# A list scheduler that orders a fused attention and two-MoE kernel: own-engine waits, separate small tasks and a mode for turned blocks

## The chip, the cores and the metric

The kernel runs on one core of a Trainium2 chip. The metric is device time in microseconds (us) of one execution; lower is better. In the profile PE is the matmul engine, PEld its weight loads, DVE the vector engine, ACT the scalar engine, POOL GpSimd and SP the engine that issues most of the DMAs.

## The reference

Block-causal attention (blocks of 64) feeds a layer of three maxima, and that feeds a routed mixture of experts:

```python
# attention: B, H, S, D = 4, 8, 576, 64
scores = np.where(block_i >= block_j, scale * (q @ k.T), -1e9)
attn = np.exp(scores - scores.max(-1)); attn /= attn.sum(-1) + 1e-9
x = heads_side_by_side(attn @ v)                   # 2304 x 512
# first layer, d_ff 768
h = np.maximum(np.maximum(x @ w1, x @ w2), x @ w3)
x = h @ w_out
# second layer: 8 experts, 1024 wide, one expert for each token with x @ w_skip > 0
out = x; out[do] = x[do] + gate * (np.maximum(x[do] @ w1[e], 0) @ w2[e])
```

## The kernel before

The 2304 tokens are cut into six chunks of 384. For each chunk the attention runs in units: one pair of heads (four pairs) and one run of up to 128 query rows. A unit's steps are `s_scores` (PE, scores into `sc`), `s_max` (DVE, negated row maxima into `nm`), `s_exp` (ACT, `p` and its sums), `s_sum` (DVE, reciprocal of the sums into `r`), `s_norm` (ACT or DVE, `p` times `r`), `s_trans` (PE, blocks of `p` turned by a product with the identity, into `tp`), `s_turned` (copy of `tp` into `pT`), `s_pv` (PE, into `pv`) and `s_out` (ACT and DVE, the high and low part of `x`). Each product of the first layer is made of three float32r products of high and low parts. Per chunk it is 18 groups `mh` of 12 matmuls into `ps_h`, three groups `my` of 18 into `ps_y`, and routing (`ps_l`, `ps_r`, `ps_k`). The first layer's weights arrive as 64-bit words in 24 pieces. Each piece is decoded once: `ab` on ACT, four steps `dec` on DVE of which each reads what the one before wrote, then `hi` (ACT) and `lo` (DVE). The last six pieces are `w_out`; each is also turned (`pswt`) and multiplied by the routing weights (`psw`).

The attention of chunk c+1 is woven into the first layer of chunk c. So the program falls into: attention of chunk 0 alone; first layer of chunk 0 with the decoding and the attention of chunk 1; first layers of chunks 1 to 4 with the attention of chunks 2 to 5; first layer of chunk 5, while the first expert weights are loaded (`load_raws`) and split into high and low parts (lines 1032 and 1036); then the experts.

All but the last two parts are ordered by the class `Plan`: `build` describes each step as a `Task` with its engine, a duration, a due time `at` and what it needs; `order` plays the list through, engine by engine, and the tasks are then emitted in order of planned start. Each engine's queue runs in that order on the chip. The tables that the planner has of waits are `LATE` (from a task's end to a task on another engine) and `TURN` (when PE changes between full tiles F, two row halves R of `s_scores` and two column halves C of `s_pv`). The planner decides at each step by

```python
s, t = min(((s, t) for s, t in cand if s <= first + 0.05), key=lambda x: x[1].at)
```

Of the kernel before, what the change touches and what calls it, by code (L numbers as in the profile page):

```python
# [8 lines left out]
F32 = mybir.dt.float32  # L9
# [49 lines left out]
class Plan:  # L59
# [3 lines left out]
    TURN = {("F", "R"): 0.10, ("R", "F"): 0.10, ("F", "C"): 0.11, ("C", "F"): 0.15, ("C", "R"): 0.15, ("R", "C"): 0.2}  # L63
# [11 lines left out]
    def ready(self, t, eng):  # L75
        when = 0.0
        for d in t.deps:
            if d.end is None:
                return None
            when = max(when, d.end + (0.0 if d.on == eng else self.LATE[d.on]))  # L80
        for name in t.acq:
            n = len(self.allocs[name]) + t.acq.count(name) - self.bufs[name]
            for k in range(max(n - t.acq.count(name), 0), n):
                for d in self.allocs[name][k].releases_of[name]:
                    if d.end is None:
                        return None
                    when = max(when, d.end + (0.0 if d.on == eng else self.LATE[d.on]))
        return when

    def order(self):  # L90
# [14 lines left out]
        while todo:  # L105
            best = None
            for e in free:
                first, cand = None, []
                for t in todo:
                    if e in t.eng:  # L110
                        r = self.ready(t, e)
                        if r is not None:
                            s = max(r, free[e])
                            cand.append((s, t))
                            first = s if first is None else min(first, s)
                if first is None:
                    continue
                s, t = min(((s, t) for s, t in cand if s <= first + 0.05), key=lambda x: x[1].at)
                if best is None or s < best[0]:
                    best = (s, t, e)  # L120
# [6 lines left out]
            if e == "PE":  # L127
                t.end += self.TURN.get((mode, t.mode), 0.0)
                mode = t.mode
# [24 lines left out]
def build(S, E, groups, units):  # L154
# [14 lines left out]
    for u in units:  # L169
# [3 lines left out]
        when.append((c - 1) * span + (-6 if c == 0 else 0) + 0.8 * span * n / per[c])  # L173
# [27 lines left out]
    for ks in su:  # L201
# [9 lines left out]
        for n, k in enumerate(ks):  # L211
# [6 lines left out]
            mx = S.add("DVE", one * (parts if sets == 2 else 1) + 0.07 * parts, at - 2, lambda k=k: E.mx(k), [sc])  # L218
# [6 lines left out]
            rs = S.add("DVE", 0.16, at - 3, lambda k=k: E.rs(k), exs)  # L225
            nms = []
            for j in range(sets):
                nm = S.add(dict(ACT=0.19 + 0.83e-3 * nk, DVE=0.13 + 0.52e-3 * nk), 0, at - 2.5 + 0.1 * j, None, [rs])
# [4 lines left out]
            for m in range(0, todo, 4):  # L233
# [3 lines left out]
                           ["tp"] + (["pT"] if m == 0 else []))  # L237
# [43 lines left out]
    for k in range(18 + NF):  # L281
        at = first_w + w_pace * k if k < 18 else 8 + 5.0 * (k - 18)
# [132 lines left out]
def _moe1_phase(tc, nc, const, small, g):  # L415
# [11 lines left out]
    with ExitStack() as st_y:  # L427
# [187 lines left out]
        def s_sum(k):  # L615
# [8 lines left out]
            nc.vector.reciprocal(r[:, 0:sets], r[:, 0:sets])  # L624
# [50 lines left out]
        E.load, E.load_v, E.sc, E.mx, E.ex, E.rs, E.nm = load, load_v, s_scores, s_max, s_exp, s_sum, s_norm  # L675
# [622 lines left out]
```

## Time and profile before

| | |
|---|---|
| median of 3 runs | 664.79 us (664.69 to 665.62) |
| profiled execution | 664.43 us, span of its instructions 662.6 us |
| around the span | 1.83 us |
| PE busy | 616.7 us (93%) |
| DVE busy | 388.5 us (59%) |
| ACT busy | 325.4 us (49%) |
| mean granted TensorE clock | 0.971 |

PE is busy nearly throughout. The granted clock is 1.0 (2.4 GHz) in most of the span and 0.5 (1.2 GHz) in some stretches. A busy share over the whole span mixes parts that differ: decoding of weights happens in the first 130 us alone.

### The profile page before, as it was taken

How to read it: one execution, taken by the hardware profiler on the slowest of the kernel's cores; microseconds unless marked ns; L12 is line 12 of the kernel's file. 1: busy time of each engine (PE TensorE's matmuls, PEld its weight loads, DVE VectorE, ACT ScalarE, POOL GpSimd, SP SyncE). 2: the span in 40 equal slices, each digit the busy share in tenths (PEclk: the TensorE clock that was granted, in tenths of full speed). 3: DMA queues.
4: the chain of work that ended last, by engine and by line, in shares of the span. 5: the costliest groups of instructions: out<-in, count | busy, mean ns of one | idle time of the engine just before them, and what ended most of it. 6: DMA issues, size and time to landing. Idle time of an engine off the chain costs nothing.

```text
span 662.6 us, 11537 instructions
## 1 busy us (share of the span) xinstructions
PE 616.7 (93%) x4180; PEld 513.7 (78%) x4180; DVE 388.5 (59%) x1027; ACT 325.4 (49%) x806; POOL 51.0 (8%) x101
## 2 busy tenths in 40 slices
PE   6889988899999999999999999999999993999993
PEld 4558867678888789987888878888789972787772
DVE  4999999934654444645466545664426631248891
ACT  4876766723554454533354433554436310258780
POOL 1000000002000010001000002000010012112320
PEclk9999997799999999999999999999999996999997
DMA  6466454223011120103311222000019575028930
GB/s 182 112 195 185 134 162 138 77 76 91 22 42 45 56 95 20 40 13 97 85 45 30 64 85 90 24 15 21 34 65 335 177 281 144 26 73 282 370 140 11
DMA packets 59351, 69.18 MB, mean 104 GB/s; under 512 B 7716, under 2 KB 40740, under 8 KB 59280
## 3 DMA queue, kind: packets, MB, share of 16 engines
q1 hardware_dynamic: 56336, 64.68, 30.7%
q0 software_dynamic: 1904, 3.61, 1.9%
q8 instruction: 37, 0.61, 0.4%
q14 instruction: 34, 0.28, 0.1%
q10 hardware_dynamic: 1040, 0.01, 0.1%
HBM read 57.59 MB, written 11.44 MB: 104 GB/s over the span
## 4 chain that ended last, share of the span: by engine, by line
PE 61%; DVE 15%; issue 13%; DMA 6%; ACT 2%; SPq 1%; POOL 1%; POOLq 0%; another core or an unknown queue 0%; ACTq 0%; DVEq 0%
PE ps_h L688 26%; PE ps_y L729 10%; PE sc L574 8%; PE pv L663 7%; PE tp L644 7%; DMA out_dram<-xo,ti 3%; DVE dec L485 2%; DVE dec L483 2%; PE ps_l L711 2%; DVE nm L596 1%; DVE w L500 1%; DVE dec L481 1%; DVE dec L479 1%; DVE hm L697 1%; ACT p L612 1%
## 5 line engine op out<-in xcount | busy, mean ns | idle before, releaser
L688 PE MATMUL ps_h<-x,w 128*128 128x384 f32 x1296 | 246.8, 341 | 4.6 <-DVE hm L697 2.6
L688 PEld LDWEIGHTS ps_h<-x,w 128*128 128x128 f32 x1296 | 222.1, 188 | 14.0 <-issue 5.2
L612 ACT ACTIVATE p<-sc,nm 128x288 f32<-128x288 f32 (+6 forms) x168 | 84.8, 512 | 40.6 <-DVE nm L601 34.9
L649 ACT COPY pT<-tp 128x512 f32<-128x512 f32 (+2 forms) x100 | 49.6, 509 | 55.8 <-PE tp L644 55.4
L574 PE MATMUL sc<-k,q 64*64 64x288 f32 (+9 forms) x384 | 69.0, 460 | 8.5 <-DMA q<-in_kq_dram 4.9
L644 PE MATMUL tp<-cst_sb,p 128*128 128x128 f32 x432 | 67.3, 287 | 5.6 <-DVE x L671 2.0
L644 PEld LDWEIGHTS tp<-cst_sb,p 128*128 128x128 f32 x432 | 51.7, 146 | 19.7 <-issue 6.6
L663 PE MATMUL pv<-pT,vt 128*64 128x128 f32 (+1 forms) x960 | 62.6, 274 | 2.9 <-ACT pT L649 2.8
L663 PEld LDWEIGHTS pv<-pT,vt 128*64 128x64 f32 x960 | 49.7, 140 | 17.6 <-issue 8.6
L596 DVE TENSOR_REDUCE nm<-sc 128x2 f32<-128x256 f32 (+7 forms) x64 | 51.9, 812 | 11.8 <-PE sc L581 10.7
L574 PEld LDWEIGHTS sc<-k,q 64*128 64x128 f32 (+1 forms) x384 | 30.2, 183 | 26.1 <-issue 10.1
L729 PE MATMUL ps_y<-wo_h,h_h 128*128 128x512 f32 x108 | 44.7, 414 | 0.0
L1036 DVE TENSOR_TENSOR lo<-raw,hi 128x1024 fp32r<-128x1024 f32 x34 | 40.4, 1218 | 5.4 <-ACT hi L1032 4.3
L729 PE MATMUL ps_y<-wo_h,h_l 128*128 128x512 f32 x108 | 42.9, 397 | 0.0
L729 PE MATMUL ps_y<-wo_l,h_h 128*128 128x512 f32 x108 | 42.7, 395 | 0.0
L649 DVE COPY pT<-tp 128x512 f32<-128x512 f32 (+2 forms) x36 | 19.6, 546 | 36.6 <-PE tp L644 36.0
L632 DVE TENSOR_SCALAR p<-p,r 128x576 f32<-128x576 f32 (+8 forms) x95 | 36.0, 395 | 5.9
L671 DVE TENSOR_TENSOR x<-pv,x 128x128 fp32r<-128x128 f32 (+1 forms) x80 | 20.5, 273 | 32.2 <-ACT x L673 31.6
L734 ACT COPY y<-ps_y 128x512 f32<-128x512 f32 x18 | 10.6, 587 | 56.3 <-PE ps_y L729 50.2
L697 DVE TENSOR_TENSOR hm<-ps_h,ha 128x384 f32<-128x384 f32 x36 | 20.0, 554 | 30.6 <-PE ps_h L688 25.6
L1032 ACT CAST hi<-raw 128x1024 fp32r<-128x1024 f32 x34 | 34.4, 1052 | 4.3 <-DMA raw<-in_m_w_dram 2.6
L630 ACT ACTIVATE p<-p,r 128x576 f32<-128x576 f32 (+7 forms) x49 | 29.7, 607 | 12.5 <-DVE r L624 11.5
(161 smaller groups left out, 785.8 us busy)
## 6 DMA issues: line engine op xcount, KB each, us to landing
raw<-in_m_w_dram SPq DMA_DIRECT2D x17, 1024.0 KB, 7.1
raw<-in_w_dram SPq DMA_DIRECT2D x18, 512.0 KB, 4.0
vt<-in_v_dram SPq DMA_DIRECT2D x16, 320.0 KB, 3.5
x<-y SPq DMA_DIRECT2D x18, 256.0 KB, 2.1
out_dram<-y SPq DMA_DIRECT2D x18, 256.0 KB, 2.3
xa<-in_m_w_dram SPq DMA_DIRECT2D x4, 1024.0 KB, 6.6
raw<-in_w_out_dram SPq DMA_DIRECT2D x6, 512.0 KB, 3.5
xb<-in_m_w_dram SPq DMA_DIRECT2D x3, 1024.0 KB, 6.9
```

Source lines behind the costliest of these rows:

```text
L574: nc.tensor.matmul(bank[:, 0:hi - lo], gd["q"][rows, q0:q0 + nq], gd["k"][rows, lo:hi], start=True, stop=packed or hi != nk)
L596: nc.vector.tensor_reduce(nm, first_ps[:, :, 0:w], axis=AX.X, op=ALU.max, negate=True)
L612: nc.scalar.activation(u["p"][:, j, lo:hi], src, AF.Exp, bias=u["nm"][:, j:j + 1], scale=0.125, accum_out=u["su"][:, n, j:j + 1])
L630: nc.scalar.activation(pt, pt, AF.Copy, scale=r)
L632: nc.vector.tensor_scalar(pt, pt, r, None, op0=ALU.mult)
L644: nc.tensor.transpose(tp[:, n, :], u["p"][:, j, t * P:(t + 1) * P], ident)
L649: copy(u["pT"][:, m:m + z], u["tp", m][:, 0:z])
L663: nc.tensor.matmul(pv[64 * j:64 * j + 64, 0:nq], vt[:, t, 64 * j:64 * j + 64], pT, start=(t == 0), stop=(t == nkt - 1))
L688: nc.tensor.matmul(ps, a[:, d, :], x[:, d, :], start=(n == 0), stop=(n == 3 * ND - 1))
L729: nc.tensor.matmul(ps, a[:, f, hs], x[:, f, :], start=(n == 0), stop=(n == 3 * NF - 1))
L1032: self.nc.scalar.copy(self.w(q)[0][:, r], self.raw_of(q)[:, r])
L1036: self.nc.vector.tensor_tensor(lo[:, r], self.raw_of(q)[:, r], hi[:, r], op=ALU.subtract)
```

## The change

`OWN` adds a planned wait where a task depends on one of its own engine (0.115 us on DVE, 0.13 on ACT). The combination of two maxima, the scaling of `nm` and the reciprocal become tasks of their own (`m2`, `ms`, `rs`), so that other tasks may stand between them. Turned blocks of attention get a mode T of PE, with new `TURN` values; `STAY` prefers tasks in PE's present mode by 1 us of due time. The normalization of chunk 1's units may only run on ACT. Due times of attention units (0.7 for 0.8) and of the six `w_out` pieces (16 + 3k for 8 + 5k) move. The instructions are the same; only engine and place of some differ.

```diff
     LATE = {"PE": 0.20, "ACT": 0.15, "DVE": 0.13, "POOL": 0.15, "SP": 0.0}
-    TURN = {("F", "R"): 0.10, ("R", "F"): 0.10, ("F", "C"): 0.11, ("C", "F"): 0.15, ("C", "R"): 0.15, ("R", "C"): 0.2}
+    OWN = {"PE": 0.0, "ACT": 0.13, "DVE": 0.115, "POOL": 0.1, "SP": 0.0}
+    TURN = {"FT": 0.02, "FR": 0.11, "FC": 0.11, "TF": 0.11, "TR": 0.1, "TC": 0.1,
+            "RF": 0.18, "RT": 0.07, "RC": 0.07, "CF": 0.24, "CT": 0.15, "CR": 0.15}
+    STAY = 1.0
...
-            when = max(when, d.end + (0.0 if d.on == eng else self.LATE[d.on]))
+            when = max(when, d.end + (self.OWN if d.on == eng else self.LATE)[d.on])
...
-                s, t = min(((s, t) for s, t in cand if s <= first + 0.05), key=lambda x: x[1].at)
+                s, t = min(((s, t) for s, t in cand if s <= first + 0.05), key=lambda x: x[1].at - (self.STAY if e == "PE" and x[1].mode == mode else 0.0))
...
-        when.append((c - 1) * span + (-6 if c == 0 else 0) + 0.8 * span * n / per[c])
+        when.append((c - 1) * span + (-6 if c == 0 else 0) + 0.7 * span * n / per[c])
...
-            mx = S.add("DVE", one * (parts if sets == 2 else 1) + 0.07 * parts, at - 2, lambda k=k: E.mx(k), [sc])
+            mx = S.add("DVE", one * (parts if sets == 2 else 1), at - 2, lambda k=k: E.mx(k), [sc])
+            if parts == 2:
+                mx = S.add("DVE", 0.07, at - 2.5, lambda k=k: E.m2(k), [mx])
+            mx = S.add("DVE", 0.07, at - 2.5, lambda k=k: E.ms(k), [mx])
...
-            rs = S.add("DVE", 0.16, at - 3, lambda k=k: E.rs(k), exs)
+            rs = S.add("DVE", 0.07, at - 3, lambda k=k: E.ra(k), exs)
+            rs = S.add("DVE", 0.08, at - 3, lambda k=k: E.rs(k), [rs])
...
-                nm = S.add(dict(ACT=0.19 + 0.83e-3 * nk, DVE=0.13 + 0.52e-3 * nk), 0, at - 2.5 + 0.1 * j, None, [rs])
+                nm = S.add(dict(ACT=0.19 + 0.83e-3 * nk, **(dict(DVE=0.13 + 0.52e-3 * nk) if c != 1 else {})), 0, at - 2.5 + 0.1 * j, None, [rs])
...
-                           ["tp"] + (["pT"] if m == 0 else []))
+                           ["tp"] + (["pT"] if m == 0 else []), mode="T")
...
-        at = first_w + w_pace * k if k < 18 else 8 + 5.0 * (k - 18)
+        at = first_w + w_pace * k if k < 18 else 16 + 3.0 * (k - 18)
...
-                nc.vector.tensor_reduce(nm, first_ps[:, :, 0:w], axis=AX.X, op=ALU.max, negate=True)
...
-            nc.vector.tensor_scalar(nm[:, 0:sets], nm[:, 0:sets], 0.125, None, op0=ALU.mult)
+        def s_max_scale(k):
+            nm = ud[k]["nm"][:, 0:ud[k]["sets"]]
+            nc.vector.tensor_scalar(nm, nm, 0.125, None, op0=ALU.mult)
...
-            nc.vector.reciprocal(r[:, 0:sets], r[:, 0:sets])
+        def s_recip(k):
+            r = ud[k]["r"][:, 0:ud[k]["sets"]]
+            nc.vector.reciprocal(r, r)
```

The queue of DVE in the first layer of chunk 0 stood like this before (the number behind a name is the tile: `dec_897`, `dec_941` and `dec_980` are three pieces):

```order
L479 TENSOR_SCALAR dec_897<-dec_897 128x512
L481 TENSOR_SCALAR dec_897<-dec_897 128x512
L697 TENSOR_TENSOR hm1_943<-ps_h_904,ha_918 128x384
L483 SCALAR_TENSOR_TENSOR dec_897<-raw_843,dec_897 128x512
L485 SCALAR_TENSOR_TENSOR dec_897<-raw_843,dec_897 128x512
L623 TENSOR_SCALAR r_952<-su_922 128x2
L624 RECIPROCAL r_952<-r_952 128x2
L697 TENSOR_TENSOR hm2_958<-ps_h_927,hm1_943 128x384
L479 TENSOR_SCALAR dec_941<-dec_941 128x512
L500 TENSOR_TENSOR w5_115<-dec_897,w5_115 128x512
```

At about the same place, the first layer's weights `w4` and `w5`, it now stands like this:

```order
L486 TENSOR_SCALAR dec_865<-dec_865 128x512
L634 SCALAR_TENSOR_TENSOR r_915<-su_878 128x1
L488 TENSOR_SCALAR dec_865<-dec_865 128x512
L641 RECIPROCAL r_915<-r_915 128x1
L490 SCALAR_TENSOR_TENSOR dec_865<-raw_801,dec_865 128x512
L507 TENSOR_TENSOR w4_114<-dec_821,w4_114 128x512
L492 SCALAR_TENSOR_TENSOR dec_865<-raw_801,dec_865 128x512
L601 TENSOR_REDUCE nm_933<-sc_891 128x2
L715 TENSOR_TENSOR hm2_946<-ps_h_902,hm1_889 128x384
L507 TENSOR_TENSOR w4_114<-dec_865,w4_114 128x512
```

Three times above, and never below, an instruction stands right behind the one whose result it reads. From the program's first instruction to the last `lo` of `w_out`, instructions on DVE that so follow the one they read (same tile, partial tiles of `p` and `x` not counted) go from 123 to 19: 51 to 7 ahead of the first that reads `ps_h`, 72 to 12 behind it. Normalizations on DVE in the same stretch go from 31 to 14, on ACT from 12 to 32.

Ahead of the first `ps_y` the queue of PE ended with these rows (attention of chunk 1 and the last `pswt`):

```order
L644 MATMUL tp<-cst_sb,p 128x128 x5
L574 MATMUL sc<-k,q 64x64 x2
L663 MATMUL pv<-pT,vt 64x128 x4
L506 MATMUL pswt<-cst_sb,dec 128x128 x4
L663 MATMUL pv<-pT,vt 64x64 x2
L729 MATMUL ps_y<-wo_h,h_h 128x512
```

It now ends with these; the product of 448 columns belongs to chunk 2, and so does one of 320 columns shortly before it:

```order
L581 MATMUL sc<-k,q 128x448 x2
L588 LDWEIGHTS mask_q
L588 MATMUL sc<-mask_k,mask_q 128x64
L588 LDWEIGHTS mask_q
L588 MATMUL sc<-mask_k,mask_q 128x64
L513 MATMUL pswt<-cst_sb,dec 128x128 x4
L661 MATMUL tp<-cst_sb,p 128x128 x5
L747 MATMUL ps_y<-wo_h,h_h 128x512
```

Chunk 2's first scores have moved ahead of `ps_y`. At the end of the planned part the last `pv` of the attention stood behind the last `ps_y` of chunk 4 and the first matmul of chunk 5:

```order
L729 MATMUL ps_y<-wo_l,h_h 128x512
L688 MATMUL ps_h<-x,w_110 128x384
L663 MATMUL pv<-pT,vt 64x128 x10
L688 MATMUL ps_h<-x,w_110 128x384 x23
L688 MATMUL ps_h<-x,w_111 128x384 x24
```

It now stands ahead of the count `ps_k` and of the last 18 `ps_y` of chunk 4:

```order
L747 MATMUL ps_y<-wo_h,h_h 128x512
L747 MATMUL ps_y<-wo_h,h_l 128x512
L747 MATMUL ps_y<-wo_l,h_h 128x512
L680 MATMUL pv<-pT,vt 64x128 x10
L804 LDWEIGHTS ones
L804 MATMUL ps_k<-cum_69,ones 128x8
```

On PE, changes between kinds of tile that aren't full (R and C) and anything else number 184 before and 186 now, up to the last `ps_y` of chunk 4; those between full tiles and turned blocks go from 112 to 103.

## Rows read from the trace of the kernel before

**Rows 1.** Page, busy tenths and granted clock in 40 slices of 16.6 us.

```profile
PE   6889988899999999999999999999999993999993
...
DVE  4999999934654444645466545664426631248891
...
PEclk9999997799999999999999999999999996999997
```

**Rows 2.** Busy time by stage (--windows), columns in its first line.

```profile
core 0: us, PE busy (x) PEld busy (x) DVE busy (x) ACT busy (x) POOL busy (x), PEclk, DMA share, GB/s
0.00:42.35 42.35, 31.34 (x236) 18.96 (x236) 31.87 (x108) 28.98 (x92) 1.90 (x12) 1.00 0.54 154
42.35:131.97 89.62, 81.47 (x586) 66.97 (x585) 85.20 (x216) 60.60 (x147) 1.83 (x11) 0.92 0.49 145
131.97:155.03 23.06, 23.03 (x139) 17.57 (x137) 7.33 (x38) 6.30 (x20) 3.47 (x6) 0.92 0.26 81
155.03:489.90 334.87, 333.72 (x2489) 286.54 (x2486) 175.39 (x538) 154.93 (x446) 18.29 (x47) 1.00 0.17 50
489.90:534.20 44.30, 41.94 (x249) 39.46 (x249) 23.35 (x31) 18.39 (x26) 0.27 (x6) 1.00 0.64 226
```

**Rows 3.** Chain that ended last, 42 to 155 us: shares, then pieces (start, length).

```profile
by line: PE ps_y L729 13.0%; DVE dec L485 10.9%; DVE dec L483 10.6%; DVE w L500 6.9%; DVE dec L481 5.2%; DVE hm L697 5.2%; DVE dec L479 5.1%; issue 4.4%; PE tp L644 4.4%; PE pv L663 4.2%; DVE nm L596 3.9%; PE sc L574 3.6%; DVE nm L591 2.5%;
...
60.24 0.69 DVE dec L485
60.94 0.47 DVE hm L697
```

**Rows 4.** Timeline of DVE, 56 to 66 us: start, length, instruction.

```profile
58.13 0.42 DVE L479 TENSOR_SCALAR dec<-dec 128x512 f32<-128x512 f32 x1
58.58 0.43 DVE L481 TENSOR_SCALAR dec<-dec 128x512 int32<-128x512 int32 x1
...
61.32 0.42 DVE L479 TENSOR_SCALAR dec<-dec 128x512 f32<-128x512 f32 x1
61.66 0.68 DVE L500 TENSOR_TENSOR w<-dec,w 128x512 fp32r<-128x512 f32 x1
```

**Rows 5.** Norms by shape on DVE (0 to 132 us) and ACT (0 to 155).

```profile
L632 DVE TENSOR_SCALAR p<-p,r 128x512 f32<-128x512 f32 x4 | 1.9, 484 | 0.2
L630 ACT ACTIVATE p<-p,r 128x512 f32<-128x512 f32 x4 | 2.9, 718 | 0.1
```

**Rows 6.** Two stretches of PE by granted clock (us, PE busy, PEclk, DMA).

```profile
108.20:115.10 6.90, 6.12 (x38) 0.51 0.28 59
...
125.30:135.60 10.30, 10.25 (x48) 0.50 0.23 65
```

**Rows 7.** Timeline of PE from 155 us.

```profile
155.03 4.44 PE L688 MATMUL ps_h<-x,w 128*128 128x384 f32 x24
159.30 0.82 PE L644 MATMUL tp<-cst_sb,p 128*128 128x128 f32 x6
159.88 2.35 PE L688 MATMUL ps_h<-x,w 128*128 128x384 f32 x12
162.07 1.03 PE L644 MATMUL tp<-cst_sb,p 128*128 128x128 f32 x8
```

**Rows 8.** Waits of PE, 155 to 490 us: in total, times, longest.

```profile
PE tp L644 <- DVE p L632: 0.9, 2, 0.4
```

**Rows 9.** Timeline of PE at the last chunk's first layer.

```profile
490.20 1.31 PE L663 MATMUL pv<-pT,vt 128*64 128x128 f32 x20
...
495.92 8.62 PE L688 MATMUL ps_h<-x,w 128*128 128x384 f32 x48 [0.22 <-ACT ha L693]
505.85 6.36 PE L688 MATMUL ps_h<-x,w 128*128 128x384 f32 x35 [1.31 <-DVE hm L697]
```

**Rows 10.** Chain that ended last, 484 to 560 us.

```profile
497.39 5.32 DMA raw<-in_m_w_dram
...
504.10 1.23 DVE lo L1036
```

More of the change, by code (lines that the diff above doesn't have):

```diff
@@ L86, in ready @@
                         return None
-                    when = max(when, d.end + (0.0 if d.on == eng else self.LATE[d.on]))
+                    when = max(when, d.end + (self.OWN if d.on == eng else self.LATE)[d.on])
         return when
@@ L127, in order @@
             if e == "PE":
-                t.end += self.TURN.get((mode, t.mode), 0.0)
+                t.end += self.TURN.get(mode + t.mode, 0.0)
                 mode = t.mode
@@ L586, in s_max @@
             u = ud[k]
-            parts, sets, first_ps = u["parts"], u["sets"], u["first"]
+            parts, first_ps = u["parts"], u["first"]
             nm = u["nm"] = sm.tile([P, 2], F32, tag="nm", name="nm")
@@ L592, in s_max @@
                                         negate=True)
-                if len(parts) == 2:
-                    nc.vector.tensor_tensor(nm[:, 0:1], nm[:, 0:1], nm[:, 1:2], op=ALU.min)
             else:
@@ L597, in s_max, with s_max2 @@
                 if len(parts) == 2:
-                    nm2 = sm.tile([P, 2], F32, tag="nm2", name="nm2")
-                    nc.vector.tensor_reduce(nm2, u["ps"][:, :, 0:w], axis=AX.X, op=ALU.max, negate=True)
-                    nc.vector.tensor_tensor(nm, nm, nm2, op=ALU.min)
-            nc.vector.tensor_scalar(nm[:, 0:sets], nm[:, 0:sets], 0.125, None, op0=ALU.mult)
+                    u["nm2"] = sm.tile([P, 2], F32, tag="nm2", name="nm2")
+                    nc.vector.tensor_reduce(u["nm2"], u["ps"][:, :, 0:w], axis=AX.X, op=ALU.max, negate=True)
+        def s_max2(k):
+            nm = ud[k]["nm"]
+            if ud[k]["packed"]:
+                nc.vector.tensor_tensor(nm[:, 0:1], nm[:, 0:1], nm[:, 1:2], op=ALU.min)
+            else:
+                nc.vector.tensor_tensor(nm, nm, ud[k]["nm2"], op=ALU.min)
+        def s_max_scale(k):
+            nm = ud[k]["nm"][:, 0:ud[k]["sets"]]
+            nc.vector.tensor_scalar(nm, nm, 0.125, None, op0=ALU.mult)
         def s_exp(k, j):
@@ L673, in s_out @@
                 nc.scalar.copy(xh, pv)
-        E.load, E.load_v, E.sc, E.mx, E.ex, E.rs, E.nm = load, load_v, s_scores, s_max, s_exp, s_sum, s_norm
+        E.load, E.load_v, E.sc, E.mx, E.ex, E.ra, E.rs = load, load_v, s_scores, s_max, s_exp, s_sum, s_recip
+        E.m2, E.ms, E.nm = s_max2, s_max_scale, s_norm
         E.tp, E.ev, E.pv = s_trans, s_turned, s_pv
```

## The prediction

> **What bounds the kernel now.** I read the page's slices first. PE is at 9 almost throughout, but the first eight slices (132 us) have 6 and 8 in them, and DVE stands at 9 in seven of these eight and nowhere else in the planned part [rows 1]. The granted clock dips in slices 7 and 8. So the next view is busy time by stage, cut at the first `ps_h` (42.35 us), the first `ps_y` (131.97), the end of chunk 0's first layer (155.03), the end of the last planned `ps_y` (489.9) and the last chunk's first `ps_y` [rows 2]. The reader is to see four things in it:
>
> - 0 to 42.35 us: PE is idle for 42.35 - 31.34 = 11.0 us.
> - 42.35 to 131.97: PE idle 89.62 - 81.47 = 8.15 us, while DVE is busy 85.20 of 89.62 (95%) and ACT 60.60 (68%).
> - 155 to 490: PE idle 334.87 - 333.72 = 1.15 us. There is nothing to win on the other engines here.
> - The last chunk: PE idle 44.30 - 41.94 = 2.36 us.
>
> Third view, the chain that ended last: between 42 and 155 us its shares by line are, beside PE's `ps_y` (which comes last), those of DVE: the decoding steps, the splits `w`, the maxima; its pieces lie end to end on DVE [rows 3]. That stage ends when DVE has done its queue; PE follows. Fourth, PE's clock: it was 0.5 from 108.2 to 115.1 and again from 125.3 to 135.6 us (1.2 GHz), with PE busy 6.12 and 10.25 us in them [rows 6]. Work at half clock takes twice the time, so half of the busy time is lost: (6.12 + 6.67)/2 = 6.4 us up to 131.97 (where the second drop is 6.67 us old and PE busy in all of it), and half of the other 3.6 us, 1.8, behind it. The idle time of this stage lies around these drops.
>
> What could be won in the first 155 us without less work on PE is therefore 11.0 + 8.15 + 6.4 + 1.8 = 27.4 us. The instructions don't change, so PE's work doesn't either; the question is how much of these 27.4 us goes, and what new waits come.
>
> **The change part by part.**
>
> *Waits on the own engine.* In the timeline of DVE the second decoding step starts 58.58 - 58.13 = 0.45 us behind the first when it stands right behind it, but when another instruction stands there, that one starts 61.66 - 61.32 = 0.34 us behind the same first step [rows 4]. So an instruction that reads its predecessor's result costs about 0.12 us more. The same first step lasts 0.42 us in both cases; the difference is in when the next may begin. The order shows 123 such places up to the last `lo` of `w_out` before and 19 now: 44 fewer ahead of the first `ps_h`, 60 fewer behind it. That is 44 x 0.12 = 5.3 us and 60 x 0.12 = 7.2 us of DVE's time.
>
> Here a rule of the Trainium skill speaks against the change. "VectorE: DVE Perf Modes", section "The DRAIN you can't avoid", says that the next operation doesn't start until the pipe has emptied, that this holds behind each operation and that a semaphore between costs nothing extra. By that rule the 0.12 us wouldn't depend on what stands behind, and these two terms would be nothing. The trace disagrees, 0.45 against 0.34 us for one and the same predecessor. It stays a rival below.
>
> *Normalizations moved to ACT.* 17 fewer on DVE up to the last `lo` (31 to 14), 7 of them ahead of the first `ps_h` and 10 behind it. A norm of 512 columns takes 0.48 us on DVE and 0.72 us on ACT [rows 5]. For the sizes that move (64 to 576) I take half of the 512's price for the 7 small ones, 7 x 0.25 = 1.8 us, and 0.35 for the other 10, 3.5 us; the bounds are 17 times nothing (if DVE isn't what ends) and 17 x 0.48 = 8.2. ACT gets 20 more (12 to 32), at most 20 x 0.72 = 14 us. It is busy 28.98 + 60.60 = 89.6 us of 132, so it would be busy 104 of about 119: 87%, below the 95% at which DVE now runs. So I cost ACT's share at nothing on the path. If it did land there, a norm on ACT ends 0.24 us later than on DVE, 20 x 0.24 = 4.8 us.
>
> *The start (0 to 42.35).* DVE gives up 5.3 + 1.8 = 7.1 us. It is busy 31.87 of 42.35 (75%), so about three quarters of what it gives up moves the first `ps_h`: 5 us. Bounds: 2 (the loads and the first scores set the pace) and 7.
>
> *First layer of chunk 0 (42.35 to 131.97).* DVE's need falls to 85.20 - 7.2 - 3.5 = 74.5 us. PE's need is 81.47 - 6.4 = 75.1 us at full clock, and chunk 2's first scores with what comes with them now stand ahead of `ps_y`, which makes some 4 us more of it (that is taken from the stages behind). So PE becomes the longer one, by little, and each waits for the other. The fullest engine in this part of the trace was 95% busy; at 95%, PE's 79 us take 83, so 4 us of idle are left in place of 8.15. Without the long waits I expect no clock drop: 6.4 us. Gain 8.15 - 4 + 6.4 = 10.5 us; bounds 4 (a clock drop all the same) and 14.5 (no idle). By that the first `ps_y` is at 42.35 - 5 + 83 = 120 us.
>
> *Behind it.* 1.8 us of half clock up to 135.6 go with the drop.
>
> *Turns of PE.* Groups of 12 matmuls into `ps_h` take 2.14 us each when they follow each other (4.27 for 24) and 2.19 between turned blocks [rows 7]: a full tile's change to turned blocks and back costs about 0.05 us. There are 9 changes fewer, 0.2 us. The changes to and from the half tiles of scores and `pv` are 184 and 186; at ten times 0.05 the two would cost 1 us, and I take nothing. So the new table of turns and `STAY` are worth about 0.2 us here.
>
> *Steady part (155 to 490).* PE waits there 0.9 us in total for turned blocks that aren't normalized yet [rows 8]. DVE and ACT are busy about half of it, so that freeing them changes nothing. Zero, with 1.15 us as the most that can be won.
>
> *Last chunk.* The first expert weights load when the attention's last `x` is done. Its `pv` ran at 490.20, behind the last `ps_y`; the first load began at 497.39, its split on DVE at 504.10, the maximum queued behind that split ended PE's wait at 505.85, of 1.31 us [rows 9, 10]. Now that `pv` stands ahead of 18 `ps_y`, so the loads begin some 5 us sooner against the matmuls. The waits of 1.31 and 0.22 us go: 1.5 us. The rest of the 2.36 us, and the experts' part, stay. Loads of keys and of weights share SP's queue in a new order; a load behind another that waits for a buffer would be the way in which the start loses again.
>
> *Sum.* 5 + 10.5 + 1.8 + 0.2 + 1.5 = 19.0 us. The profiled execution has 664.43 us, its span 662.6 and 1.83 us around it that stay; 664.43 - 19.0 = 645.4. The median of the runs is 664.79, 0.36 us more. I say **645 us**.
>
> **The rivals.**
>
> 1. *The clock falls all the same.* Three engines near 90% leave gaps on PE, and behind similar gaps the clock fell twice. For it: small products of the routing weights stand in that stretch, as before. Against it: up to 42 us PE was idle for 11 us at a granted 1.00 [rows 2]. It gives back 6.4 + 1.8 = 8.2 us: 653.5.
>
> 2. *DVE isn't relieved by the order* (the rule of the flush). Then only the norms and the last chunk's start are left: 664.43 - 1.8 - 3.5 - 1.5 - 0.2 = 657.4. Against it stand the two distances in [rows 4].
>
> 3. *No change.* DVE is busy but what ends the stage is the arrival of weights; then the order of DVE's queue moves nothing and the time stays within 0.2% (about what a measurement of this kernel can tell from no change), 664. Against it: the chain there is on DVE [rows 3].
>
> 4. *Slower: turned blocks wait.* PE now takes the turned blocks of a unit as soon as its plan allows, preferring the mode in which it is, and the norms of chunk 1 are late on ACT. In the steady part PE has no slack. Half of the 103 changes are from full tiles to turned blocks, some 52; if each waited 0.4 us, as the longest did [rows 8], that is 21 us, more than the 19 won: 667. It decides from 19/52 = 0.37 us a group. Against it: only 0.9 us of such waiting exists, and the freed DVE makes norms earlier, not later.
>
> **How the numbers follow.** Forecast 0.64, own range 639 to 651 (bounds of the terms: with the largest values 7 + 14.5 + 1.8 + 2.4 + 1.2 = 27, 637; with the small ones 2 + 8 + 1.8 + 1 = 13, 651). Clock 0.17, flush 0.06, no change 0.04, slower 0.09. Faster by over 0.2% is 0.64 + 0.17 + 0.06 = 0.87, same 0.04, slower 0.09. The range 638 to 656 holds the forecast and the clock's case, 0.81.
>
> **What would show it.** Right: the first `ps_h` at about 37 us, the first `ps_y` at about 120, granted clock 1.0 from 17 us to the last chunk's end, first and second decoding steps that no longer stand 0.45 us apart, PE idle of about 4 us in chunk 0's first layer and no more than 2 from there to the last chunk, and no wait over 0.5 us behind the split of the first expert weights. Wrong: DVE still 95% busy up to the first `ps_y` (2), clock at 0.5 around it (1), waits of turned blocks on norms by the dozen behind 140 us (4), or PE waiting for loads of keys in the first 40 us.

## The result and the profile after

The changed kernel takes 646.04 us (median of 4 runs, 645.92 to 647.57) beside 664.74 us of the kernel before on the same chip (4 runs): a ratio of 0.9723, 95% interval 0.9705 to 0.9742. The profiled execution has 646.17 us, its span 644.3. Ratios here leave out an execution that took over 1.5% longer than the fastest of its kernel.

The page's slices, busy tenths and granted clock, answer to [rows 1]:

```profile
PE   6799999999999999999999999999999985999992
...
DVE  4999999625554256562555634655437431268980
...
PEclk9999999999999999999999999999999995999996
```

PE is at 9 from the third slice on, where 8s stood up to the eighth; DVE leaves its row of 9s a slice sooner; the clock's dip in slices 7 and 8 is gone, and the first one left is behind the last chunk's first layer. Busy time by stage, cut at the same matmuls as [rows 2] (columns: the stage and its length, busy time and instructions of PE, PEld, DVE, ACT and POOL, granted clock, DMA share, GB/s):

```profile
0.00:41.36 41.36, 30.95 (x237) 18.63 (x237) 31.46 (x109) 31.84 (x101) 1.90 (x12) 1.00 0.61 169
41.36:120.10 78.74, 76.58 (x623) 65.21 (x621) 76.05 (x207) 65.26 (x169) 2.45 (x13) 1.00 0.56 169
120.10:138.41 18.31, 18.31 (x115) 14.61 (x112) 6.01 (x31) 7.78 (x22) 0.07 (x1) 1.00 0.24 77
138.41:471.70 333.29, 333.29 (x2499) 286.06 (x2496) 166.36 (x523) 155.41 (x446) 20.66 (x51) 1.00 0.16 49
471.70:514.98 43.28, 40.47 (x229) 38.47 (x228) 23.22 (x30) 18.00 (x25) 0.81 (x7) 1.00 0.65 232
```

The span is 18.3 us shorter. The first `ps_h` comes 1.0 us sooner. From there to chunk 1's first `ps_h` it takes 97.05 us (41.36 to 138.41) where it took 112.68: 15.6 us, which is nearly all of the gain. PE's idle time in it is 2.16 us in place of 8.2, and none of it runs at half clock, where 8.2 us were lost before [rows 6]. That is 6.0 and 8.2 us; the other 1.4 are busy time of PE, which comes to 94.9 us in the two stages where [rows 2] give 104.5, or 96.3 without the 8.2. Why it is less isn't shown. The steady part gives 1.6 us, the last chunk 1.0, and what follows it takes 0.9 longer (128.4 to 129.3 us).

The chain that ended last between 41 and 138 us, shares by line, was DVE's work in [rows 3]:

```profile
by line: PE ps_h L706 40.5%; PE ps_y L747 12.7%; PE sc L581 9.3%; PE pv L680 8.7%; PE tp L661 8.1%; ACT p L626 2.4%; PE ps_l L729 2.3%; PE psw L522 1.8%; ACT pT L666 1.7%; issue 1.7%; PE pswt L513 1.5%; DVE dec L490 1.2%; ACT dec L478 1.2%;
```

It is PE's own work now. DVE's timeline in this stage (start, length), beside [rows 4]:

```profile
69.87 0.42 DVE L486 TENSOR_SCALAR dec<-dec 128x512 f32<-128x512 f32 x1
70.20 0.69 DVE L507 TENSOR_TENSOR w<-dec,w 128x512 fp32r<-128x512 f32 x1
70.81 0.42 DVE L488 TENSOR_SCALAR dec<-dec 128x512 int32<-128x512 int32 x1
71.14 0.15 DVE L609 TENSOR_TENSOR nm<-nm 128x1 f32<-128x1 f32 x1
```

Another instruction stands behind each decoding step, and starts 0.33 us behind it. It isn't a matter of decoding steps alone. In the trace of the kernel before, up to 135 us, nearly all close pairs on DVE fall into two groups: an instruction that reads the result of the one ahead starts 0.03 us behind that one's end, one that doesn't starts 0.08 us ahead of it. That is 0.12 us, whether the first of the two lasts 0.16 or 0.74 us.

### The profile page after: what moved, and what is told of

Its sections match the earlier page's. It is cut to its first block, busy times and chain, and to the rows that moved or that the text cites. A ratio compares the mean times of both kernels' runs of the same rounds, so it can differ in the third digit from the quotient of the medians.

```text
span 644.3 us, 11529 instructions
## 1 busy us (share of the span) xinstructions
PE 604.1 (94%) x4180; PEld 506.8 (79%) x4180; DVE 368.5 (57%) x996; ACT 334.4 (52%) x837; POOL 51.1 (8%) x101
## 4 chain that ended last, share of the span: by engine, by line
PE 71%; issue 12%; DMA 6%; DVE 3%; ACT 3%; SPq 1%; POOL 1%; POOLq 0%; another core or an unknown queue 0%; ACTq 0%
PE ps_h L706 34%; PE ps_y L747 10%; PE sc L581 9%; PE pv L680 8%; PE tp L661 7%; DMA out_dram<-xo,ti 4%; PE ps_l L729 2%; ACT p L626 1%; DMA raw<-in_m_w_dram 1%; DMA table<-pair,sloti 1%; PE ps_r L762 1%; DVE nm L601 1%; ACT pT L666 1%; SPq L988 1%; DMA x<-y 0%
## 5 line engine op out<-in xcount | busy, mean ns | idle before, releaser
L706 PE MATMUL ps_h<-x,w 128*128 128x384 f32 x1296 | 244.1, 340 | 2.8 <-DVE hm L715 2.4
L626 ACT ACTIVATE p<-sc,nm 128x288 f32<-128x288 f32 (+7 forms) x168 | 84.7, 514 | 27.2 <-DVE nm L615 26.5
L666 ACT COPY pT<-tp 128x512 f32<-128x512 f32 (+2 forms) x106 | 52.2, 505 | 56.2 <-PE tp L661 55.3
L661 PE MATMUL tp<-cst_sb,p 128*128 128x128 f32 x432 | 65.5, 280 | 3.9 <-ACT pT L666 1.8
L661 PEld LDWEIGHTS tp<-cst_sb,p 128*128 128x128 f32 x432 | 49.8, 142 | 16.7 <-issue 6.6
L680 PE MATMUL pv<-pT,vt 128*64 128x128 f32 (+1 forms) x960 | 60.4, 270 | 1.6 <-ACT pT L666 1.5
L647 ACT ACTIVATE p<-p,r 128x512 f32<-128x512 f32 (+8 forms) x74 | 42.9, 597 | 8.7 <-DVE r L641 8.1
L752 ACT COPY y<-ps_y 128x512 f32<-128x512 f32 x18 | 10.5, 586 | 56.2 <-PE ps_y L747 45.5
L623 POOL MEMSET p<- 128x128 f32 (+1 forms) x48 | 9.2, 196 | 338.3 <-PE tp L661 222.4
L715 DVE TENSOR_TENSOR hm<-ps_h,hm 128x384 f32<-128x384 f32 x36 | 20.0, 555 | 27.7 <-PE ps_h L706 27.0
L690 ACT CAST x<-pv 128x128 fp32r<-128x128 f32 (+1 forms) x80 | 20.0, 259 | 29.9 <-PE pv L680 29.4
```

The source lines that it names most:

```text
L626: nc.scalar.activation(u["p"][:, j, lo:hi], src, AF.Exp, bias=u["nm"][:, j:j + 1], scale=0.125, accum_out=u["su"][:, n, j:j + 1])
L647: nc.scalar.activation(pt, pt, AF.Copy, scale=r)
L661: nc.tensor.transpose(tp[:, n, :], u["p"][:, j, t * P:(t + 1) * P], ident)
L666: copy(u["pT"][:, m:m + z], u["tp", m][:, 0:z])
L680: nc.tensor.matmul(pv[64 * j:64 * j + 64, 0:nq], vt[:, t, 64 * j:64 * j + 64], pT, start=(t == 0), stop=(t == nkt - 1))
L706: nc.tensor.matmul(ps, a[:, d, :], x[:, d, :], start=(n == 0), stop=(n == 3 * ND - 1))
```

## The experiments

All start from the changed kernel unless it says otherwise. "Neighbours" are instructions on DVE that stand right behind the one whose result they read, up to the last piece of `w_out`, counted with partial tiles: 134 before, 25 in the changed kernel. The theory (A): the order frees DVE of its own waits, DVE no longer ends chunk 0's first layer, PE does, and its clock stays up. The main rival (D): the norms moved to ACT free DVE.

### Own wait and norms undone

```diff
-    OWN = {"PE": 0.0, "ACT": 0.13, "DVE": 0.115, "POOL": 0.1, "SP": 0.0}
+    OWN = {"PE": 0.0, "ACT": 0.0, "DVE": 0.0, "POOL": 0.0, "SP": 0.0}
...
-                ... **(dict(DVE=0.13 + 0.52e-3 * nk) if c != 1 else {}) ...
+                ... DVE=0.13 + 0.52e-3 * nk ...
```

> The changed kernel with the wait on the own engine counted as zero again and with chunk 1's norms allowed on DVE again; separate tasks, due times, turns and STAY stay as changed. Its order has 118 dependent neighbours on DVE up to the last piece of w_out (before 134, changed 25) and 33 norms there (31, 14). Theory A (DVE is relieved by order and norms, PE then ends the stage): nearly all is lost, 660 us (655 to 665), first ps_y near 131 us, clock at 0.5 around it again. Rival B (due times, turns and STAY carry the gain): 646 to 650, first ps_y near 121. Rival C (split tasks carry it, since other work can stand between): 650 to 655.

Measured: 665.8 us, ratio 1.0025 (1.0003 to 1.0047) to the kernel before; more than my 660, and just above its range. First `ps_y` at 138.45. Its first layer of chunk 0, in the same columns:

```profile
41.04:138.45 97.41, 89.68 (x620) 72.27 (x619) 90.59 (x234) 63.90 (x160) 2.10 (x12) 0.89 0.47 140
```

DVE is busy 90.59 of 97.41 us and PE idle for 7.7 again; the clock was at 0.5 from 117.1 to 141.0 us. All of the gain is gone, although due times, turns, `STAY` and the separate tasks are still there. Rivals B and C fall: by themselves these bring nothing.

### Own wait alone undone

The first of the two edits, without the second.

> The changed kernel with the wait on the own engine counted as zero, and chunk 1's norms still kept off DVE: 112 dependent neighbours up to the last piece of w_out in place of 25, 19 norms on DVE there in place of 14. Beside the kernel with both undone (665.8 us, 118 neighbours, 33 norms) it shows what the norms bring when DVE is not relieved by order. Theory A: 87 x 0.12 is 10 us of DVE, less 14 norms that stay on ACT: 657 us (653 to 661), one drop of the clock. Rival D (norms carry the gain): 650 or less. Rival E (norms are worth nothing either way): 663 to 667.

Measured: 665.3 us, ratio 1.0014 (0.9997 to 1.003), first `ps_y` at 137.74. Keeping 14 norms off DVE changes nothing against the run above. Rival E holds here, and my 657 was wrong by the price that I gave the norms, and by the clock, which was at 0.5 from 118.6 to 142.5 us and for 3.4 us from 87.9.

### Norms undone

The second edit, without the first.

> The changed kernel with chunk 1's norms allowed on DVE again, all else as changed: 21 norms on DVE up to the last piece of w_out in place of 14, 24 on ACT in place of 32, 19 dependent neighbours. Theory A: 7 norms of some 0.45 us are 3 us of DVE, which was 97% busy, so up to 3 us later: 648.5 us (646 to 650). Rival D (the norms on ACT are the main part of the gain): 655 or more. Rival E (ACT is as full as DVE, so that where the norms run is worth nothing): 646, within 0.2%.

Measured: 649.67 us, ratio 0.9771 (0.9736 to 0.9806), runs from 646.76 to 652.25. PE's idle time from the first `ps_h` to the first `ps_y` is 80.04 - 78.93 = 1.1 us, no more than in the changed kernel. What differs is the clock. The profiled execution (651.73) has a stretch at half clock:

```profile
42.38:122.42 80.04, 78.93 (x615) 68.30 (x613) 76.80 (x211) 62.26 (x159) 2.33 (x12) 0.94 0.56 164
113.50:127.15 13.65, 13.57 (x58) 11.14 (x59) 6.92 (x26) 6.08 (x19) 0.41 (x2) 0.50 0.24 64
```

Half of 13.57 is 6.8 us, more than the 5.6 by which this execution is slower than the changed kernel's. The fastest run, 646.76, has a mean clock of 0.984, like the changed kernel's runs (0.981 to 0.986). So with DVE relieved by order the norms' engine is worth nothing on DVE's side. My 648.5 came close by luck: I had worked it out from a fuller DVE, and it was the clock. Rival D falls.

### The own wait alone, on the kernel before

The kernel before with `OWN` and with `m2`, `ms` and `rs` as tasks of their own; no new `TURN`, no mode T, no `STAY`, no norm kept off DVE, old due times.

> The kernel before with the separate tasks and the counted own wait alone; due times, turns, modes and chunk 1's norms as before. 23 dependent neighbours on DVE up to the last piece of w_out, 25 norms there. Theory A: the order alone brings most of it, 650 us (646 to 654), first ps_y near 123 us, clock without or with one drop. Rival D (norms): 657 or more. Rival B (due times, turns): 660 or more.

Measured: 648.39 us, ratio 0.9759 (0.9729 to 0.9789).

```profile
0.00:39.76 39.76, 30.09 (x230) 18.29 (x230) 29.75 (x106) 28.83 (x93) 1.89 (x12) 1.00 0.60 165
39.76:119.44 79.68, 75.16 (x602) 64.08 (x600) 78.37 (x212) 61.70 (x155) 1.93 (x11) 1.00 0.54 162
```

The counted wait with the separate tasks brings 2.4 of the 2.8% alone, and a first `ps_h` that is sooner than the changed kernel's. The clock stayed up although PE was idle for 4.5 us in this stage.

`OWN` counts ACT's wait too (0.13 us), and the two were not undone apart. But the order took away pairs on DVE alone: by the names of the tiles, without their numbers (which counts some pairs too many), readers right behind what they read number 152 on DVE and 13 on ACT up to the first `ps_y` before, 59 and 12 here, 49 and 21 in the changed kernel.

### Decoding steps in one task

```diff
-        for n, dur in enumerate((0.335, 0.335, 0.6, 0.6)):
-            d = S.add("DVE", dur, at, lambda k=k, n=n: E.dec(k, n), [d])
+        d = S.add("DVE", 2.215, at, lambda k=k: [E.dec(k, n) for n in range(4)], [d])
```

> The changed kernel with the four decoding steps of a tile as one task again, so that they stand one behind the other and no other work can stand between; its duration is the sum of the four. The same instructions; 91 dependent neighbours on DVE up to the last piece of w_out in place of 25, 66 more. Theory A (0.12 us for each, paid on DVE): 7.9 us more of DVE, of which most ends the stage: first ps_y 5 to 8 us later, 652 us (649 to 655), 6 more if the clock falls; decoding steps 0.45 us apart. Rival F (what counts is not the wait but which work the plan puts first): 646 to 648, first ps_y near 121.

Measured: 654.76 us, ratio 0.9855 (0.983 to 0.9879); that is 8.7 us more than the changed kernel's 646.04. Its timeline of DVE, and two stretches:

```profile
60.70 0.43 DVE L485 TENSOR_SCALAR dec<-dec 128x512 f32<-128x512 f32 x1
61.16 0.43 DVE L487 TENSOR_SCALAR dec<-dec 128x512 int32<-128x512 int32 x1
61.62 0.69 DVE L489 SCALAR_TENSOR_TENSOR dec<-raw,dec 128x512 int32<-128x512 int32 x1
```

```profile
0.00:47.01 47.01, 33.04 (x230) 19.94 (x231) 34.73 (x113) 32.11 (x96) 1.90 (x12) 0.93 0.59 167
30.01:33.42 3.41, 3.41 (x18) 2.35 (x17) 3.31 (x10) 2.65 (x9) 0.00 (x0) 0.50 0.43 148
```

The steps stand 0.46 us apart again, and rival F's 646 to 648 is out. But the price isn't that of the 66 waits alone. 5.6 us lie ahead of the first `ps_h` (47.01), where the clock fell twice and where this plan also put more of the decoding (28 instructions on DVE for 23, 3.9 us; rows in the account of the start, below). By chunk 1's first `ps_h`, when all decoding is done, the kernel is 9.7 us later (148.15 for 138.41); the clock's falls, with a third from 57.3 to 60.7, are up to 5.0 us of it. So the neighbours' own share lies between 4.8 and 9.7 us, and so do the 7.9 expected. A long task also keeps short work waiting: PE's scores waited 6.0 us for ACT's `p` up to 48 us, for 1.5 in the changed kernel. This run doesn't part that from the waits.

### Turns as before

```diff
-    TURN = {"FT": 0.02, "FR": 0.11, "FC": 0.11, "TF": 0.11, "TR": 0.1, "TC": 0.1,
-            "RF": 0.18, "RT": 0.07, "RC": 0.07, "CF": 0.24, "CT": 0.15, "CR": 0.15}
-    STAY = 1.0
+    TURN = {("F", "R"): 0.10, ("R", "F"): 0.10, ("F", "C"): 0.11, ("C", "F"): 0.15, ("C", "R"): 0.15, ("R", "C"): 0.2}
+    STAY = 0.0
...
-                t.end += self.TURN.get(mode + t.mode, 0.0)
+                t.end += self.TURN.get((mode, t.mode), 0.0)
...
-                           ["tp"] + (["pT"] if m == 0 else []), mode="T")
+                           ["tp"] + (["pT"] if m == 0 else []))
```

> The changed kernel with the turns of the kernel before: no mode of their own for turned blocks, the old table, no STAY. 296 changes of mode on PE in place of 289. Theory A (turns are worth 0.2 us): 646 us (645.5 to 647.5), steady part from chunk 1's first ps_h to chunk 5's within 1 us of 333.3. Rival G (turns are the source of the 1.6 us that the steady part lost, and of some of PE's smaller busy time): 648 to 650, steady part 335 or more.

Measured: 652.87 us, ratio 0.9822 (0.9794 to 0.9849), runs from 649.8 (mean clock 0.981) to 654.25 (0.973). In the profiled execution of 651.0 the steady part has 334.68 us, 1.4 more than in the changed kernel; PE is idle for 3.4 us ahead of the first `ps_y`, and the clock fell for 3.4 us. By time rival G is nearer than I was. But the kernel with the own wait alone has the old turns too, and its steady part takes 333.29 us. So the turns aren't what shortens it; this order came out 1% worse, and why stays open.

### Due times as before

```diff
-        when.append((c - 1) * span + (-6 if c == 0 else 0) + 0.7 * span * n / per[c])
+        when.append((c - 1) * span + (-6 if c == 0 else 0) + 0.8 * span * n / per[c])
...
-        at = first_w + w_pace * k if k < 18 else 16 + 3.0 * (k - 18)
+        at = first_w + w_pace * k if k < 18 else 8 + 5.0 * (k - 18)
```

> The changed kernel with the due times of the kernel before (attention spread over 0.8 of a chunk, w_out's pieces at 8 + 5.0 k). Theory A: due times only change which work goes first, PE's work stays: 646 us (645 to 648.5). Rival B (earlier attention and w_out in one go bring the first ps_y forward): 652 or more, first ps_y after 126 us.

Measured: 647.53 us (median of five), ratio 0.9742 (0.9708 to 0.9775), runs from 644.97 to 648.24 (a sixth, at a mean clock of 0.964, 655.82). The first `ps_y` comes at 116.9, 3.2 us sooner, and the last chunk's first layer takes 45.29 us, 2.0 more. No difference in sum, as expected.

### Chunk 0's norms on DVE

```diff
-                nm = S.add(dict(ACT=0.19 + 0.83e-3 * nk, ...
+                nm = S.add(dict(DVE=0.13 + 0.52e-3 * nk) if c == 0 else dict(ACT=0.19 + 0.83e-3 * nk, ...
```

> The changed kernel with chunk 0's norms on DVE alone: 24 on DVE and none on ACT in the start, before 14 and 12 up to there. It asks why the first ps_h came only 1 us sooner. Theory S1 (ACT, 95% busy from 15 us on, has become what ends the start, through the norms moved to it): first ps_h at 39 to 40 us, total 644 to 645. Rival S2 (DVE, 94% busy, still ends it): 10 norms of 0.35 us more, first ps_h at 44 to 45, total 648 to 650. Rival S3 (neither: loads of keys and PE's own chain end it): first ps_h within 0.7 us of 41.4.

Measured: first `ps_h` at 39.13, total 652.93 us, ratio 0.983 (0.9806 to 0.9854). From 15 us to the first `ps_h`, in the changed kernel and then in this one:

```profile
15.00:41.36 26.36, 21.82 (x195) 13.19 (x191) 24.86 (x82) 25.04 (x79) 0.15 (x1) 1.00 0.58 162
```

```profile
15.00:39.13 24.13, 20.99 (x188) 12.72 (x184) 22.23 (x80) 19.28 (x63) 0.14 (x1) 1.00 0.54 151
...
39.13:123.83 84.70, 82.11 (x612) 68.46 (x611) 79.47 (x214) 67.67 (x172) 2.10 (x12) 0.93 0.54 160
101.90:111.90 10.00, 9.07 (x97) 7.09 (x95) 9.93 (x36) 9.20 (x30) 0.56 (x3) 1.00 0.67 186
111.92:125.57 13.65, 12.97 (x64) 10.75 (x65) 8.47 (x28) 8.44 (x27) 0.74 (x4) 0.50 0.28 81
```

The first `ps_h` came where theory S1 had it: ACT was busy 25.04 of 26.36 us (95%) in the changed kernel and is at 80% here, and the first `ps_h` is 2.2 us sooner. But ACT isn't shown to be the cause. DVE has ten norms more and still 2.6 us less to do in this stretch, since the plan put decoding off: 15 of its instructions (7.90 us) lie ahead of the first `ps_h`, where the changed kernel has 23 (11.98 us; rows in the account of the start, below). So S2's premise, a fuller DVE, wasn't met, and the run doesn't tell a freed ACT from a freed DVE. The total went the other way: DVE has 3.4 us more to do behind the first `ps_h` (79.47 for 76.05), and the clock fell from 111.9 to 125.6 us, half of 12.97, 6.5 us. In the ten us ahead of that PE was idle for only 0.9.

### What lets the clock fall: two tries

The kernel above, with three of four products of `w_out` with the routing weights left out:

```diff
-            for d in range(ND):
-                nc.tensor.matmul(ps, wt_at[k][:, d, :], wr_sb[:, d, :], start=(d == 0), stop=(d == ND - 1))
+            nc.tensor.matmul(ps, wt_at[k][:, 0, :], wr_sb[:, 0, :], start=True, stop=True)
```

> The kernel with chunk 0's norms on DVE alone (652.9 us; clock at 0.5 from 111.9 to 125.6 us, PE idle only 0.9 us in the ten before), with the same order, but three of the four products of each w_out piece with the routing weights (psw, 10 columns) left out; that part of the computation is missing. PE has some 0.8 us less to do at each of six places, so its gaps can only grow. Theory H1 (the clock falls behind these small products, not behind gaps): no 0.5 ahead of the last chunk, first ps_y at 115 to 118 us, 644 to 646 us. Rival H2 (it falls behind gaps): the drop stays, first ps_y at 120 to 124, 649 to 653.

Its total (1175 us) says nothing here, since with such weights the choice of experts is another one, and what lies behind the last chunk's first layer takes 649 us for 129; what lies ahead of it can be compared.

```profile
102.10:112.10 10.00, 7.99 (x84) 5.83 (x83) 9.93 (x36) 9.15 (x30) 0.56 (x3) 1.00 0.63 185
112.10:125.75 13.65, 12.20 (x56) 9.48 (x57) 8.42 (x29) 9.24 (x30) 0.74 (x4) 0.50 0.31 84
```

The drop stays, at the same place, and the first `ps_y` is at 122.32. H1 falls as far as it makes these products necessary for it. And the changed kernel, with each of these products done twice:

```diff
-            for d in range(ND):
-                nc.tensor.matmul(ps, wt_at[k][:, d, :], wr_sb[:, d, :], start=(d == 0), stop=(d == ND - 1))
+            for n in range(2):
+                for d in range(ND):
+                    nc.tensor.matmul(ps, wt_at[k][:, d, :], wr_sb[:, d, :], start=(d == 0), stop=(d == ND - 1))
```

> The changed kernel with each product of a w_out piece with the routing weights done twice (the second overwrites the first). About 1 us more of PE at each of six places, and fewer gaps. Theory H1 (the clock falls behind these small products): it falls to 0.5 around 110 to 130 us as it doesn't in the changed kernel, first ps_y near 131, 656 us or more. Rival H2 (gaps): clock 1.0 up to the last chunk, first ps_y at 123 to 126, 649 to 652 us.

Measured: 653.98 us, ratio 0.9879 (0.9835 to 0.9922), first `ps_y` at 126.79.

```profile
110.30:120.30 10.00, 9.68 (x90) 8.10 (x89) 7.49 (x30) 7.90 (x28) 0.61 (x4) 1.00 0.40 107
120.33:127.16 6.83, 6.39 (x30) 4.30 (x31) 4.78 (x13) 3.49 (x10) 0.47 (x2) 0.50 0.17 49
```

Here it falls behind ten us with 0.3 us of idle time, so H2 falls too as the whole cause; the time lies between the two forecasts. Neither the gaps alone nor these products alone decide it.

### Two mixtures

```diff
-        when.append((c - 1) * span + (-6 if c == 0 else 0) + 0.7 * span * n / per[c])
+        when.append((c - 1) * span + (-6 if c == 0 else 0) + (0.7 if c == NCH - 1 else 0.8) * span * n / per[c])
...
-        at = first_w + w_pace * k if k < 18 else 16 + 3.0 * (k - 18)
+        at = first_w + w_pace * k if k < 18 else 8 + 5.0 * (k - 18)
```

That is the first kernel; the second has the edit of chunk 0's norms beside it.

> The changed kernel with the old due times of w_out's pieces (8 + 5 k) and the old spread of the attention (0.8) but for the last chunk, which keeps 0.7. The kernel with both old due times reached the first ps_y 3.2 us sooner and lost 2 in the last chunk. If the two parts add: 645 us (643.5 to 646), first ps_y near 117, last chunk's first layer 43.3 us. Rival I (what is won ahead of the first ps_y is work put off to the steady part, where PE has no slack): 646, no change.

> As the kernel with the mixed due times, and chunk 0's norms on DVE alone, which brought the first ps_h at 39.1 in place of 41.4 us. If the clock stays up: 643 us (641 to 645). Rival J (chunk 0's freed time on ACT goes on as a fuller DVE in the next stage, and the clock falls as in the kernel with the norms alone): 649 to 653.

Measured: the first has ratio 0.9787 (0.9736 to 0.9837), three runs between 646.4 and 648.5 and three between 655.6 and 657.7 (mean clocks 0.984 to 0.986 and 0.964 to 0.967). The second has 650.03 us, ratio 0.9789 (0.9774 to 0.9805). Both have what was meant in its stage: the last chunk's first layer at 43.1 us in the first, the first `ps_h` at 38.93 in the second. Both lose it elsewhere: the first in the steady part (335.56 us) and ahead of its first `ps_y` (119.2 us, behind a start that was 1.4 us longer), the second here:

```profile
38.93:122.96 84.03, 79.89 (x619) 66.89 (x617) 79.19 (x213) 67.90 (x170) 2.10 (x11) 0.98 0.53 157
...
140.81:476.31 335.50, 335.50 (x2509) 287.74 (x2506) 172.11 (x534) 156.38 (x452) 17.44 (x47) 1.00 0.17 50
```

PE is idle for 4.1 us ahead of its first `ps_y`, the clock fell for 3.4 us, and the steady part takes 335.5 us for 333.3. The second's time is in rival J's range, but by idle time and the steady part more than by the clock. Neither beats the changed kernel.

## Why the prediction was right in sum, and where its terms were not

| term | forecast, us | measured, us |
|---|---|---|
| start | 5 | 1.0 |
| from the first `ps_h` to chunk 1's (the 4 us of moved work cancel out) | 10.5 + 1.8 | 15.6 |
| turns, steady part | 0.2 | 1.6 |
| last chunk's first layer | 1.5 | 1.0 |
| behind it | 0 | -0.9 |
| sum | 19.0 | 18.3 |

The sum came out by compensation. The start and the last chunk gave 4.5 us less than forecast and what follows took 0.9 more; the first layer and the steady part gave 4.7 more. Some of this is a matter of which side of the first `ps_h` the same work lies on (see the start), the rest is luck. The range isn't what its terms give either: its upper end, 651, was added up with 8 us for the first layer, for which the text had 4 as the bound, with a fall of the clock in it; with 4 it would be near 656.

**Own waits: right.** 0.12 us for each neighbour is what DVE's timelines show. Undoing the edit alone gives everything back (665.3), the edit alone on the kernel before brings 648.4, and 66 neighbours put back cost 8.7 us, with the clock's falls in it. By the rival named after the Trainium skill ("VectorE: DVE Perf Modes", section "The DRAIN you can't avoid": the next operation doesn't start until the pipe is empty) the time would have been 657.4; these runs decide against that, as does the distance of 0.33 us above. The same section adds that a next operation that isn't held starts earlier; the prediction left this out, so the rival was the rule without its exception, and the exception is what DVE's instructions that don't read the result ahead of them show.

**Norms on ACT: wrong.** I took 1.8 us for the start and 3.5 for the first layer, with ACT's share "at nothing on the path". Where DVE is relieved by order, norms back on DVE add no idle time on PE (1.1 us), and where it isn't, keeping them off helps nothing (665.3 and 665.8). So nothing of the 3.5 us shows. ACT, which my 87% was worked out for over the whole 120 us, was 95% busy from 15 us on; whether that cost anything in the start isn't shown, since the run without these norms on ACT also put decoding off.

**Start: mis-sized, 1.0 for 5.** The step that failed is that what DVE gives up moves the first `ps_h`. The plan spent much of it on decoding for later. DVE's decoding steps and splits ahead of the first `ps_h` (stretch and its length, busy time and instructions, granted clock, DMA share, GB/s), in the kernel before, the changed one, the own wait alone, the own wait undone, chunk 0's norms on DVE and the decoding in one task:

```profile
0.00:42.35 42.35, 9.27 (x18) 1.00 0.54 154
0.00:41.36 41.36, 11.98 (x23) 1.00 0.61 169
0.00:39.76 39.76, 10.08 (x18) 1.00 0.60 165
0.00:41.62 41.62, 6.09 (x12) 1.00 0.55 155
0.00:39.13 39.13, 7.90 (x15) 1.00 0.59 164
0.00:47.01 47.01, 15.84 (x28) 0.93 0.59 167
```

The changed kernel has 2.7 us more of it there than the kernel before, and its first `ps_h` is still 1.0 us sooner; with the same 18 instructions the own wait alone has it 2.6 us sooner. Against the own wait undone it has 5.9 us more of decoding, and five norms fewer, in about the same time (the clock record of that execution lies late, at 19.6 us, see the last section). What was done early is missing behind the first `ps_h`, which fits the larger gain there: start and first layer together were forecast at 17.3 us and gave 16.6. PE's waits for loads of keys, one of the signs of being wrong, are no cause: 4.9 us before, 5.0 now. Whether ACT takes a share of the missing 4 us stays open.

**First layer of chunk 0: right in place, mis-sized.** The first `ps_y` came at 120.10, as forecast, but 78.74 us behind the first `ps_h` and not 83: PE had 76.6 us of work there and not the 79 that I had counted, and its idle time shrank to 2.16 us, where I had left 4. The clock's 8.2 us came as they were worked out from [rows 6].

**Clock: the forecast held, its reason didn't.** I expected no drop "without the long waits". The runs show drops with 0.3 and 0.9 us of idle time in the ten us before, and none in the kernel with the own wait alone, with 4.5 us of it in the stage. The prediction's argument against rival 1, 11 us of idle time at a granted 1.00 in the start, holds for half of it only: the first clock record of that trace lies at 16.1 us, and 5.5 of the 11.0 us lie ahead of it. So rival 1 was nearer than its place in the text: seven of the nine variants that keep the counted own wait and all products ran at 0.5 somewhere between the first `ps_h` and chunk 1's. The Trainium skill ("TensorE: Matmul & The Clock Gate", section "HAM oscillation — how this bites in real kernels") puts a fall down to long idle gaps of PE; the trace with the doubled products, with 0.3 us of idle time in the ten ahead of the fall, doesn't agree. What decides it stays open.

**Turns: their 0.2 us isn't shown.** The steady part is as long in the kernel with the own wait alone, which has the old turns; undoing the turns in the changed kernel cost 6.8 us in all, and why stays open.

**Turned blocks that wait (rival 4): didn't happen.** PE is busy 333.29 of 333.29 us in the steady part. There 1.15 us of idle time were to be had and went; the other 0.4 are within what orders differ by (332.0 to 335.6 us over all variants).

**Last chunk: the step failed.** The loads did begin 5.8 us sooner against the matmuls: 1.7 us behind the chunk's first `ps_h` (473.40), where it was 7.5 [rows 2, 10]. But the wait stayed. The chain, DVE's timeline and PE's there:

```profile
473.40 5.35 DMA raw<-in_m_w_dram
...
481.12 0.56 DVE hm L715
```

```profile
479.98 1.23 DVE L1054 TENSOR_TENSOR lo<-raw,hi 128x1024 fp32r<-128x1024 f32 x1 [3.27 <-ACT hi L1050]
481.12 0.55 DVE L715 TENSOR_TENSOR hm<-ps_h,hm 128x384 f32<-128x384 f32 x1
```

```profile
481.72 2.36 PE L706 MATMUL ps_h<-x,w 128*128 128x384 f32 x12 [1.51 <-DVE hm L715]
484.54 21.10 PE L706 MATMUL ps_h<-x,w 128*128 128x384 f32 x120 [0.46 <-ACT ha L711]
506.47 6.54 PE L706 MATMUL ps_h<-x,w 128*128 128x384 f32 x36 [0.84 <-DVE hm L715]
```

PE is idle for 2.81 us, for 2.36 before. The maximum (`hm`) still queues on DVE behind the first split (`lo`), which still waits for its load; sooner loads only meet an earlier group. The step that failed is that a sooner load takes the wait away. The 1.0 us came from work moved out of the stage: PE is busy for 1.5 us less, most of it the `pv` of 1.31 us [rows 9] that now lies in chunk 4.

## What to carry to other kernels

A list scheduler has to know what a dependent instruction on the same engine waits: 0.12 us on DVE, left out of the plan at some hundred places, was worth 2.4% here, about half of it through the clock, which no longer fell (8.2 us). Price a move between engines in the stage where it lands (ACT was 95% busy there from 15 us on), not over a mean of stages. Before reading a gain or a loss off the start of a stage, count which work a new plan has put ahead of that point. And where a stage ends by a narrow margin on PE, orders that look alike can differ by 1% through the clock alone, so that each variant has to be timed over several executions.

## What the runs showed of the hardware

PE ran at half speed up to about 16 us: four turned blocks took 1.09 us at 12.24 and 0.69 at 15.51 in the changed kernel (timeline of PE), though the views give the granted clock of this stretch as 1.00.

```profile
12.24 1.09 PE L661 MATMUL tp<-cst_sb,p 128*128 128x128 f32 x4 [0.25 <-DVE p L649]
...
15.51 0.69 PE L661 MATMUL tp<-cst_sb,p 128*128 128x128 f32 x4
```

The clock's first record, at 1.0, lies at 15.6 us there, and between 15.6 and 19.6 in the other executions. Kernels with the same instructions in the same order up to the first `ps_h` differ by it: the one with mixed due times has its record at 18.5 and its first `ps_h` at 42.75 us, those with chunk 1's norms allowed on DVE and with the doubled products at 17.9 and at 42.38 and 42.47, the one with the old due times and the changed kernel at 15.6 and at 41.34 and 41.36. Differences of up to 1.4 us in the first `ps_h` between single executions say nothing of a plan, and the 1.0 us between the kernel before (record at 16.1) and the changed one is no larger. The 2.2 us of chunk 0's norms on DVE are more than that, and its record lies at 16.3.

The clock fell behind ten us in which PE was 80, 91 and 97% busy, and not in every run of a kernel: the runs with chunk 1's norms on DVE lie between 646.8 us at a mean clock of 0.984 and 652.3 at 0.970. Nor does the order alone decide: the kernels with the old due times and with the mixed ones have the same order up to the first `ps_y` (the rest of their plans differs), and in the profiled executions the clock stayed at 1.0 in the one and fell from 107.3 to 110.7 us in the other, whose start was 1.4 us later.
